# Short transfers behind the loads, and a store of 32 rows, in a cached grouped-query attention block

## The chip, the cores and the metric

The kernel runs on one core of a Trainium2 chip. A core has five instruction streams, named in the profile as PE (matrix engine; PEld is its weight load), DVE (vector), ACT (scalar), POOL and SP. SP computes nothing here: it issues transfers between HBM and the on-chip memory (SBUF). The transfers are moved by 16 DMA engines, and ACT issues two of them as well. The matrix engine writes its sums into PSUM, which is divided into banks.

The metric is device time in microseconds (us), from the first to the last instruction and a little around it. The span of the profile is the part between the first and the last instruction that was recorded.

## The reference, cut to what matters

```
x        [8, 4, 512]          bf16     B=8 sequences of 4 new tokens
k_cache  [8, 8, 2048, 128]    bf16     B, KV heads, cached tokens, head size
v_cache  [8, 8, 2048, 128]    bf16
wq       [512, 4096]          bf16
wo       [4096, 512]          bf16

q = (x @ wq).reshape(B, 4, 32, 128).transpose(0, 2, 1, 3)     # 32 query heads
k = repeat(k_cache, 4, axis=1);  v = repeat(v_cache, 4, axis=1)
p = softmax(einsum("bhqd,bhkd->bhqk", q, k) * 128**-0.5)
o = einsum("bhqk,bhkd->bhqd", p, v)
out = o.transpose(0, 2, 1, 3).reshape(B, 4, 4096) @ wo         # [8, 4, 512]
```

K and V are 33.6 MB each, wq and wo 4.2 MB each; x and the output are 32 KB each.

## The kernel before, in words

The work is cut into eight units. A unit holds four KV heads and two sequences; `units` lists them, the four pairs of sequences of the first four heads first. For a unit, K is one block of 4 MB and V another: 128 partitions, two sequences, 16 KB for each.

All large blocks pass through `ring`, a buffer with four slots of 4 MB. The order of the blocks is the list `loads`: K0, wq, K1, V0, K2, V1, K3, ..., V5, K7, V6, V7, wo. A block takes the slot of the block four places ahead of it, so its transfer waits until that one has been used up. `issue(done)` puts transfers on SP's queue as far as slots are promised; it is called once before the loop and then at the end of each pass of it (`issue(2 + 2 * u)`). Most blocks are one transfer; K0, wq, K1, V0, V1 and V7 are two; wo (`load_wo`, L113) is seven: two of 1 MB for the first half of the rows, then 1 MB, 512 KB, 256 KB and twice 128 KB. The transfers take their turn on eight completion semaphores: each transfer has one of the eight, in order of issue, and waits on its issuing engine until the transfer that had it before has landed. On one engine transfers are issued in order; a transfer that waits holds back those behind it.

`pad` is a buffer of 192 columns ahead of the ring, which nothing reads or writes.

In the loop over units, DVE turns K blocks (`turn`, L172), PE forms the scores of all heads of the unit in `s_ps`, four banks (`scores`, L195), DVE takes the maxima (`top`, L208), ACT the exponentials (`exps`, L229), DVE transposes them (L243), and ACT and POOL (in the last unit DVE too) spread them into block-diagonal weights (`weights`, L253). PE multiplies the V block of the unit before by them (`values`, L269). The last steps of a unit bring its result into the order of tokens (`scaled`, `joined`, L287, `by_tokens`, L307, `to_rows`, L321).

At the end `project` (L332) multiplies by wo. For each of 16 rows of wo in each half, two matmuls of 256 columns add up the output: the left half of the columns on partitions 0 to 31, the right half on partitions 32 to 63, both in the first bank of `s_ps`. One ACT copy (L409) brings the 64 partitions into `out_sb`, and one transfer (L411) stores 64 rows of 512 B, with a pattern of two halves by 32 tokens by 256 columns on the side of HBM.

Of the kernel before, what the change touches and what calls it, by code (L numbers as in the profile page):

```python
# [8 lines left out]
BF16 = mybir.dt.bfloat16  # L9
# [8 lines left out]
def kernel(  # L18
# [9 lines left out]
    nc = tc.nc  # L28

    B, Sq, D = x.shape  # L30
# [4 lines left out]
    T = B * Sq  # L35
# [14 lines left out]
    DH = D // 2  # L50
# [6 lines left out]
    const = ctx.enter_context(tc.tile_pool(name="const", bufs=1))  # L57
# [10 lines left out]
    pad = ring_pool.tile([128, 192], BF16, name="pad")  # L68
# [8 lines left out]
    q_bd = [const.tile([128, NB, J * 2, G, NB, Q], BF16, name=f"q_bd{i}") for i in range(2)]  # L77
    p_bd = [const.tile([128, CH // 2, G, 32, 2], BF16, name=f"p_bd{i}") for i in range(4)]
    oP = [const.tile([128, RW, T], BF16, name=f"oP{i}") for i in range(NG)]
    out_sb = const.tile([2 * T, DH], BF16, name="out_sb")  # L80

    units = [(gg, bp) for gg in range(NG) for bp in range(NP)]
    slot_of = {}
# [2 lines left out]
    def take(key):  # L86
        slot_of[key] = n_loads[0] % NS
        n_loads[0] += 1
        return slot_of[key]

    def load_kv(kind, u, parts, engines=(nc.sync,)):

        gg, bp = units[u]
        slot = take((kind, u))
        src = (k_cache if kind == "k" else v_cache)[NB * bp : NB * bp + NB, G * gg : G * gg + G]
        rows = src.rearrange("b g (s c) d -> (g s) b (c d)", c=C)
        n = C * Dh
        for i, (b0, b1, h0, h1) in enumerate(parts):
            h0, h1 = int(h0 * n), int(h1 * n)
            engines[i % len(engines)].dma_start(ring[:, slot, b0:b1, h0:h1], rows[:, b0:b1, h0:h1])  # L100

    def load_wq():
        slot = take("wq")
        rows = wq.rearrange("(p b r) n -> p b (r n)", b=NB, r=R // NB)
        for b, engine in enumerate((nc.sync, nc.scalar)):
            engine.dma_start(ring[:, slot, b, :], rows[:, b])

    def load_wo():
        slot = take("wo")
        for gg, cuts in ((0, (0, 8, RW)), (1, (0, 8, 12, 14, 15, RW))):  # L110
            rows = wo[gg * G * 512 : (gg + 1) * G * 512, :].rearrange("(p r) j -> p (r j)", r=RW)
            for r0, r1 in zip(cuts, cuts[1:]):
                nc.sync.dma_start(ring[:, slot, gg, r0 * D : r1 * D], rows[:, r0 * D : r1 * D])  # L113

    whole = [(0, NB, 0, 1)]
    by_sequence = [(b, b + 1, 0, 1) for b in range(NB)]
    by_half = [(0, NB, 0, 0.5), (0, NB, 0.5, 1)]
    loads = ["k0", "wq", ("k", 1)]
# [7 lines left out]
    def issue(done):  # L126

        while loads and n_loads[0] < done + NS:
            what = loads.pop()
            if what == "k0":  # L130
                load_kv("k", 0, by_sequence, (nc.sync, nc.scalar))
                nc.sync.dma_start(x_sb[:, :], x.flatten_outer_dims())
            elif what == "wq":
                load_wq()
            elif what == "wo":
                load_wo()
            elif what in (("k", 1), ("v", 0), ("v", 1)):
                load_kv(*what, by_sequence)
            else:
                load_kv(*what, by_half if what == ("v", NU - 1) else whole)  # L140

    issue(0)

    make_identity(nc, ident[:])
# [6 lines left out]
    for r, b in ((r, b) for r in range(rep) for b in range(NB)):  # L151
        nc.gpsimd.tensor_copy(
            out=perm[:, r, 32 - NB * Sq :]
            .rearrange("k (g x) -> k g x", g=G)[:, :, : NB * Sq]
            .rearrange("k g (b s) -> k b g s", b=NB)[:, b],
            in_=by_row[:, r, b],
        )
    for b in range(NB):
        nc.vector.tensor_reduce(
            out=of_b[:, b : b + 1],  # L160
            in_=ident[:, :].rearrange("k (g b q) -> k b g q", g=G, b=NB)[:, b],
# [27 lines left out]
    s_ps = psum_s.tile([128, NT, 512], FP32, name="s_ps")  # L189
# [138 lines left out]
    def project(gg, r0, r1):  # L328
        w = ring[:, slot_of["wo"], gg, :].rearrange("p (r j) -> p r j", r=RW)
        for r in range(r0, r1):  # L330
            for half in range(2):
                nc.tensor.matmul(  # L332
                    out_ps[half * T : (half + 1) * T, :],
                    lhsT=oP[gg][:, r, :],
                    rhs=w[:, r, half * DH : (half + 1) * DH],
                    start=(gg == 0 and r == 0),
                    stop=(gg == NG - 1 and r == RW - 1),
                )
# [9 lines left out]
    for gg in range(NG):  # L348
        psq = psum_o.tile([128, rep * Dh], FP32, tag="o", name="psq")
        for r in range(R):  # L350
# [10 lines left out]
            out=q_sb[:, gg, :, :, :, :].rearrange("t r j w e -> t (r j w e)"), in_=psq[:, :]  # L361
        )
        for i in range(rep):
            nc.vector.transpose(  # L364
                out=qT[:, gg, :, :, i, :, :].rearrange("w j b s e -> w j b (s e)").bitcast(FP32),
                in_=q_sb[:, gg, i, :, :, :].rearrange("t j w e -> t (j w e)").bitcast(FP32),
            )
    queries(0)

    out_ps = s_ps[: 2 * T, 0, :DH]  # L370
    for u in range(NU + 1):
        if u < NU:
            for t in range(NT):
# [19 lines left out]
        if u >= 1:  # L393
# [5 lines left out]
            if u == NU:  # L399
                joined(u - 1)  # L400
                by_tokens(u - 2)
        issue(2 + 2 * u)
    project(0, 0, 4)
    by_tokens(NU - 1)
    to_rows(NG - 1, RW // 4)
    project(0, 4, RW)
    project(1, 0, RW)
    assert not loads
    nc.scalar.copy(out=out_sb[:, :], in_=out_ps)  # L409
    rows = out.flatten_outer_dims().rearrange("t (h n) -> h t n", h=2)  # L410
    nc.sync.dma_start(out=rows, in_=out_sb[:, :])  # L411


# [28 lines left out]
```

## Time and profile before

| | us |
|---|---|
| median of 3 runs | 191.63 |
| lowest and highest run | 185.8, 191.71 |
| the profiled execution | 185.8 |
| its span | 183.9 |

| engine | busy us | share of the span |
|---|---|---|
| PE | 133.3 | 72% |
| DVE | 127.3 | 69% |
| ACT | 74.1 | 40% |
| POOL | 37.7 | 20% |

The rows of the profile name an engine, a line of the kernel, the operation and what is written and read (`out<-in`); a `q` behind the engine's name stands for its sequencer, which issues transfers and handles semaphores. A count is given as `x7`, a time of one instruction in ns, other times in us. In a table of stretches, each row gives the stretch, its length, the busy time of PE, PEld, DVE, ACT and POOL with the number of instructions, and at the end the granted clock of PE, the mean busy share of the 16 DMA engines and the GB/s that they moved.

### The profile page before, as it was taken

Reading aid. Unit: us, or ns where it says so; the run is one execution under the profiler, and the core shown is the slowest. Engines: PE = TensorE matmul, PEld = TensorE weight load, DVE = VectorE, ACT = ScalarE, POOL = GpSimd, SP = SyncE. Lnnn points to the kernel's source line nnn. Section 1 sums busy time; section 2 is a strip of 40 time slices with the busy share of each in tenths; the row PEclk is TensorE's granted clock in tenths of the full one; section 3 lists DMA queues with packets and bytes.
Section 4 is the critical chain, followed back from the end, with each engine's and each line's share of the span. In section 5 each row is a group of like instructions: output and inputs, shape, how many; then the busy total and the mean of one; then the engine's idle time right before and its main releaser. Section 6 shows DMA issues by size and latency. Waiting matters only on the chain.

```text
span 183.9 us, 2334 instructions
## 1 busy us (share of the span) xinstructions
PE 133.3 (72%) x900; PEld 81.4 (44%) x900; DVE 127.3 (69%) x160; ACT 74.1 (40%) x91; POOL 37.7 (20%) x98
## 2 busy tenths in 40 slices
PE   0000079901999699978996898789788968899991
PEld 0000023300358335833782377238633853398870
DVE  6527029068975997499749965997898579769140
ACT  2000020049506940793099009902980297037010
POOL 8700033008001700260034004300520040005000
PEclk9999999995699999999999999999999999999997
DMA  6999999999999999999999999999999999999980
GB/s 271 410 435 420 435 421 438 424 438 438 424 435 421 435 424 440 417 440 435 424 431 420 442 424 433 442 413 438 420 442 428 431 435 420 421 426 424 428 316 8
DMA packets 6109, 75.71 MB, mean 412 GB/s; under 512 B 498, under 2 KB 850, under 8 KB 1106
## 3 DMA queue, kind: packets, MB, share of 16 engines
q1 hardware_dynamic: 5810, 71.37, 91.1%
q10 hardware_dynamic: 288, 4.19, 5.4%
q8 instruction: 7, 0.11, 0.2%
q14 instruction: 4, 0.03, 0.0%
HBM read 75.53 MB, written 0.03 MB: 411 GB/s over the span
## 4 chain that ended last, share of the span: by engine, by line
DVE 37%; DMA 25%; PE 19%; ACT 9%; issue 3%; SPq 2%; POOL 2%; DVEq 0%; ACTq 0%; POOLq 0%
DVE kt L172 23%; DMA ring<-in_wo_dram 14%; PE s_ps L195 13%; DMA ring<-in_wq_dram 11%; ACT p_sb L229 8%; DVE stat L208 8%; PE o_ps L269 4%; DVE pt L243 2%; DVE stat L260 2%; PE psq L353 2%; SPq L113 2%; POOL p_bd L253 1%; DVE stat L216 1%; DVE o_sb L287 1%; POOL q_bd L184 1%
## 5 line engine op out<-in xcount | busy, mean ns | idle before, releaser
L195 PE MATMUL s_ps<-kt,q_bd 128*128 128x512 bf16 x256 | 67.4, 395 | 24.3 <-POOL q_bd L184 16.3
L172 DVE STREAM_TRANSPOSE kt<-ring 128x1024 f32<-128x1024 f32 x64 | 73.8, 1207 | 5.5 <-DMA ring<-in_k_cache_dram 5.2
L269 PE MATMUL o_ps<-ring,p_bd 128*128 128x256 bf16 x512 | 57.0, 273 | 0.0
L195 PEld LDWEIGHTS <-q_bd 128*128 128x128 bf16 x256 | 24.7, 99 | 66.1 <-issue 23.6
L269 PEld LDWEIGHTS <-p_bd 128*128 128x128 bf16 x512 | 49.8, 98 | 5.9
L229 ACT ACTIVATE p_sb<-s_ps,stat 128x1024 bf16<-128x1024 f32 x16 | 22.0, 1399 | 65.3 <-DVE stat L216 65.3
L253 ACT COPY p_bd<-pt 32x1024 bf16<-32x1024 bf16 x44 | 45.8, 1041 | 1.3 <-DVE pt L243 0.8
L253 POOL COPY p_bd<-pt 32x1024 bf16<-32x1024 bf16 x16 | 17.0, 1063 | 112.0 <-DVE pt L243 109.5
L208 DVE TENSOR_REDUCE stat<-s_ps 128x1 f32<-128x1024 f32 x16 | 18.8, 1219 | 12.2 <-PE s_ps L195 12.2
L243 DVE STREAM_TRANSPOSE pt<-p_sb 128x512 f32<-128x512 f32 x16 | 11.4, 711 | 16.1 <-ACT p_sb L229 16.0
L184 POOL COPY q_bd<-qT 32x64 bf16<-32x64 bf16 x64 | 13.1, 230 | 19.4 <-DVE qT L364 17.6
L344 PE MATMUL xtp<-ident,x_sb 32*128 32x32 bf16 x4 | 0.3, 194 | 14.1 <-DMA x_sb<-in_x_dram 14.1
L353 PE MATMUL psq<-ring,xT_sb 128*32 128x512 bf16 x32 | 3.6, 629 | 8.2 <-DMA ring<-in_wq_dram 8.2
L364 DVE STREAM_TRANSPOSE qT<-q_sb 128x64 f32<-128x64 f32 x8 | 1.2, 213 | 8.9 <-ACT q_sb L360 8.9
L146 DVE MEMSET p_bd<- 128x2048 uint32 x3 | 5.3, 1765 | 2.0 <-PEq L426 1.2
L344 PEld LDWEIGHTS <-x_sb 32*128 32x128 bf16 x4 | 0.2, 117 | 14.1 <-DMA x_sb<-in_x_dram 14.1
L260 DVE TENSOR_SCALAR stat<-of_b,stat 128x2 f32<-128x2 f32 x8 | 5.9, 733 | 0.3
L287 DVE SCALAR_TENSOR_TENSOR o_sb<-o_ps,stat,o_sb 128x128 bf16<-128x128 f32 x8 | 2.5, 316 | 4.8 <-ACT o_sb L281 4.8
L353 PEld LDWEIGHTS <-xT_sb 128*32 128x32 bf16 x32 | 1.3, 139 | 9.7 <-issue 9.2
L360 ACT CAST q_sb<-psq 128x512 bf16<-128x512 f32 x2 | 1.2, 586 | 10.9 <-PE psq L353 10.9
L281 ACT ACTIVATE o_sb<-o_ps,stat 128x128 bf16<-128x128 f32 x8 | 2.9, 368 | 5.6 <-PE o_ps L269 5.4
L347 ACT COPY xT_sb<-xtp 128x128 bf16<-128x128 bf16 x1 | 0.3, 266 | 11.5 <-PE xtp L344 11.5
(26 smaller groups left out, 38.4 us busy)
## 6 DMA issues: line engine op xcount, KB each, us to landing
ring<-in_k_cache_dram SPq DMA_DIRECT2D x6, 4096.0 KB, 22.0
ring<-in_v_cache_dram SPq DMA_DIRECT2D x5, 4096.0 KB, 25.3
ring<-in_v_cache_dram SPq DMA_DIRECT2D x6, 2048.0 KB, 27.1
ring<-in_k_cache_dram SPq DMA_DIRECT2D x3, 2048.0 KB, 25.4
ring<-in_wo_dram SPq DMA_DIRECT2D x3, 1024.0 KB, 25.6
ring<-in_k_cache_dram ACTq DMA_DIRECT2D x1, 2048.0 KB, 12.1
ring<-in_wq_dram ACTq DMA_DIRECT2D x1, 2048.0 KB, 20.2
ring<-in_wq_dram SPq DMA_DIRECT2D x1, 2048.0 KB, 20.9
```

Of the source, the lines that this page charges most:

```text
L146: nc.vector.memset(t[:, :, :, :, :], 0.0)
L172: nc.vector.transpose(out=kt[:, :, :, :, :].rearrange("w c j s e -> w (c j s e)").bitcast(FP32), in_=ring[:, slot_of["k", u], b, t * n : ( ...
L184: nc.gpsimd.tensor_copy(out=qb[rows, b, :, g, b, :].rearrange("w (j e) q -> w j e q", e=2), in_=qT[rows, gg, :, NB * bp + b, :, :, :].rear ...
L195: nc.tensor.matmul(s_ps[:, t, :], lhsT=q_bd[u % 2][:, b, 2 * j + e, :, :, :].rearrange("w g b q -> w (g b q)"), rhs=kts[u, b, t][:, :, j, ...
L208: nc.vector.tensor_reduce(out=stats[u][0][:, h : h + 1], in_=s_ps[:, 2 * h : 2 * h + 2, :].rearrange("q t n -> q (t n)"), axis=AX, op=ALU.max,
L229: nc.scalar.activation(out=p_sb[:, :, :, :].rearrange("q c s e -> q c e s"), in_=s_ps[:, 2 * h : 2 * h + 2, :].rearrange("q t (c e s) -> q ...
L243: nc.vector.transpose(out=pt[:, :, :, :].rearrange("s c q e -> s (c q e)").bitcast(FP32), in_=ps[u, h][:, :, :, :].rearrange("q c s e -> q ...
L253: copy(out=pb[rows, :, g, :, :], in_=pt[rows, :, :, :])
L260: nc.vector.tensor_scalar_mul(stats[u][3][:, :], of_b[:, :], stats[u][4][:, :])
L269: nc.tensor.matmul(o_pss[u][:, :, :], lhsT=pbs[u, h][:, i // 2, :, :, i % 2].rearrange("s g q -> s (g q)"), rhs=v[:, :, h * CH + i, :], st ...
L287: nc.vector.scalar_tensor_tensor(out=o_sb[:, 1, :], in0=o_pss[u][:, 1, :], scalar=stats[u][3][:, 1:2], in1=o_sb[:, 0, :], op0=ALU.mult, op ...
L353: nc.tensor.matmul(psq[g * T : (g + 1) * T, :], lhsT=xT_sb[:, r, :], rhs=w[:, (gg * G + g) * rep * Dh : (gg * G + g + 1) * rep * Dh], star ...
```

## The change

A list `probes` holds the numbers 1 to 16 in an order of its own. `load_rows` takes the next number n and transfers n rows of x, 12 columns (24 B) of each, into `pad`, each n to columns of its own; nothing reads them. It is called on SP behind each block from V0 to V6's (13 times: n = 8, 4, 12, 2, 6, 10, 14, 1, 3, 5, 7, 9, 11), and behind the first three pieces of wo (n = 13, 15, 16). As transfers, these take their turn on the eight completion semaphores like the others.

The right half of the output is now formed in the second bank of `s_ps`, still on partitions 32 to 63. ACT copies the left half, DVE the right half, into an `out_sb` of 32 partitions by 512 columns, and one transfer stores 32 rows of 1024 B.

```diff
-    out_sb = const.tile([2 * T, DH], BF16, name="out_sb")
+    out_sb = const.tile([T, D], BF16, name="out_sb")
...
+    probes = [16, 15, 13, 11, 9, 7, 5, 3, 1, 14, 10, 6, 2, 12, 4, 8]
+
+    def load_rows():
+
+        n = probes.pop()
+        nc.sync.dma_start(pad[:n, 12 * (n - 1) : 12 * n], x.flatten_outer_dims()[:n, :12])
+
     def load_wo():
...
             for r0, r1 in zip(cuts, cuts[1:]):
                 nc.sync.dma_start(ring[:, slot, gg, r0 * D : r1 * D], rows[:, r0 * D : r1 * D])
+                if probes:
+                    load_rows()
...
                 load_kv(*what, by_half if what == ("v", NU - 1) else whole)
+            if len(loads) < 15 and len(probes) > 3:
+                load_rows()
...
                 nc.tensor.matmul(
-                    out_ps[half * T : (half + 1) * T, :],
+                    out_ps[half],
...
-    out_ps = s_ps[: 2 * T, 0, :DH]
+    out_ps = [s_ps[h * T : (h + 1) * T, h, :DH] for h in range(2)]
...
-    nc.scalar.copy(out=out_sb[:, :], in_=out_ps)
-    rows = out.flatten_outer_dims().rearrange("t (h n) -> h t n", h=2)
-    nc.sync.dma_start(out=rows, in_=out_sb[:, :])
+    nc.scalar.copy(out=out_sb[:, :DH], in_=out_ps[0])
+    nc.vector.tensor_copy(out=out_sb[:, DH:], in_=out_ps[1])
+    nc.sync.dma_start(out=out.flatten_outer_dims(), in_=out_sb[:, :])
```

## The prediction

> **What bounds the kernel now.** I read the page's engine table and its 40 slices first.
>
> ```profile
> span 183.9 us, 2334 instructions
> PE 133.3 (72%) x900; PEld 81.4 (44%) x900; DVE 127.3 (69%) x160; ACT 74.1 (40%) x91; POOL 37.7 (20%) x98
> ...
> DMA  6999999999999999999999999999999999999980
> GB/s 271 410 435 420 435 421 438 424 438 438 424 435 421 435 424 440 417 440 435 424 431 420 442 424 433 442 413 438 420 442 428 431 435 420 421 426 424 428 316 8
> DMA packets 6109, 75.71 MB, mean 412 GB/s; under 512 B 498, under 2 KB 850, under 8 KB 1106
> ```
>
> No compute engine is busy for more than three quarters of the span, but the transfers are at nine tenths or more in 37 consecutive slices. Stretches of the trace, with the DMA share and GB/s as the last two numbers, give the steady rate:
>
> ```profile
> 60.00:140.00 80.00, 68.59 (x434) 40.86 (x433) 67.31 (x82) 43.85 (x52) 17.84 (x50) 1.00 1.00 429
> ```
>
> 75.71 MB at 429 GB/s is 176.5 us. Add the start and the tail after the last load, and the span is full. The chain that ended last, from 150 us on, says the same:
>
> ```profile
> 151.16 2.41 SPq L113
> 153.56 0.04 issue
> 153.61 25.58 DMA ring<-in_wo_dram
> 179.19 0.04 issue
> 179.23 0.62 PE s_ps L332 x6
> 179.85 0.01 issue
> 179.86 0.30 PE s_ps L332 x2
> 180.16 0.02 issue
> 180.19 0.37 ACT out_sb L409
> ```
>
> A piece of wo, issued at 153.61, lands 25.58 us later, because two V units and the rest of wo stand ahead of it. Earlier in the span the chain names DVE and PE, but those only decide when a slot comes free; the loads issued then join a backlog:
>
> ```profile
> ring<-in_k_cache_dram SPq DMA_DIRECT2D x6, 4096.0 KB, 22.0
> ring<-in_v_cache_dram SPq DMA_DIRECT2D x5, 4096.0 KB, 25.3
> ```
>
> 4096 KB take 9.8 us at 429 GB/s and land 22 to 25 us after issue, so 12 us or more of older work lies ahead of a typical load. The end is therefore set by three things: the bytes, what each of the 16 DMA engines does beside them, and the tail after 179.2.
>
> **The store.** This is the one part that I expect to gain. The tail in the timeline, and the transfers in it:
>
> ```profile
> 180.19 0.37 ACT L409 CAST out_sb<-s_ps 64x256 bf16<-64x256 f32 x1 [3.43 <-PE s_ps L332]
> 180.58 0.68 SPq L411 DMA_DIRECT2D out_dram<-out_sb  x1
> ```
>
> ```profile
> 179.60:181.80 2.20, 0.54 (x6) 0.15 (x3) 0.00 (x0) 0.37 (x1) 0.00 (x0) 1.00 0.00 0
> 181.80:182.75 0.95, 0.00 (x0) 0.00 (x0) 0.00 (x0) 0.00 (x0) 0.00 (x0) 0.56 0.13 34
> ```
>
> ```profile
> DMA packets 66, 0.03 MB, mean 27 GB/s; under 512 B 2, under 2 KB 66, under 8 KB 66
> ```
>
> The last fence counts the packets of 181.6 to 182.8: 64 rows of 512 B and two of under 512 B. A share of 0.13 of 16 engines is 2.1 engines: the old store is moved by two engines, 32 rows each, in 0.95 us, or 0.95 / 32 = 0.030 us a row. The new store has 32 rows of 1024 B and no outer count of two. On 16 engines each moves two rows; even at twice 0.030 us that is 0.12 us, and 0.83 us is saved. If it stayed on two engines, 16 rows each at 0.030 to 0.060 us would take 0.48 to 0.95 us and save 0 to 0.47. Only the large transfers, whose rows run over 128 partitions, show share 1.00 here; I side with them, since the factor of two stands in the old store's pattern alone: **-0.8 us**, bounds 0 and -0.83. The Trainium skill, "DMA: Bandwidth & Descriptors", section "Why a DMA increments its semaphore by 16 and not by 1", has a rule for it: the engines used are the largest number up to 16 that divides the outermost counts of both patterns. The 2.1 engines of the old store agree with it (counts 2 and 64).
>
> **The two copies.** The store now waits for ACT's copy and a DVE copy of the other half, side by side. Neither is in the trace in its new shape; both have near rows:
>
> ```profile
> L321 ACT CAST q_sb<-o_pm_m x2: 372/372/373, 125.3 to 176.4; 128x256 bf16<-128x256 f32 x2
> L321 DVE CAST q_sb<-o_pm_e x2: 416/420/425, 127.7 to 176.5; 128x256 bf16<-128x256 f32 x2
> ```
>
> ACT takes 372 ns for 128 partitions and 366 (0.37 above) for 64, so 32 do not make it shorter: a copy goes by its 256 columns. DVE's 420 ns ends 0.05 later: **+0.05 us**. DVE is idle by then (nothing on it in 179.60:181.80). The 64 projection matmuls stay as many, in the same order; writing two banks changes their 273 ns by nothing that I can price, bounds 0 either way, because the last eight wait for wo anyway.
>
> **The short rows.** Sixteen more transfers: 13 behind loads from the first V on (8, 4, 12, 2, 6, 10, 14, 1, 3, 5, 7, 9, 11 rows), three behind the first three pieces of wo (13, 15, 16). Together 136 rows of 24 B, 3.3 KB, nothing by bytes. Three prices remain.
>
> SP's queue. The waits of SP and its issues:
>
> ```profile
> SPq L100 <- DVE kt L172: 83.4, 8, 19.2
> SPq L100 <- PE o_ps L269: 39.0, 5, 7.9
> ...
> SPq L113 <- DMA ring<-in_v_cache_dram: 7.2, 2, 4.5
> ```
>
> ```profile
> L100 SPq DMA_DIRECT2D ring<-in_v_cache_dram x11: 328/368/554, 3.4 to 142.0; - x11
> ```
>
> Sixteen issues of 0.37 us are 5.9 us, on a queue that sits waiting for 83.4 + 39.0 us for slots. Each falls right behind a load, into such a wait, and the backlog of 12 us would hide a delay of 0.4 us in any case: **0**.
>
> New waits. The transfers take eight completion semaphores in turn, and each waits until the one eight before it has landed. With a short transfer between the loads, eight back is only four loads back. For K and V that is a load whose data has already been consumed, because the ring has four slots: no new wait. At the end it bites. The third piece of wo now waits for V6, the fourth for the first half of V7, the fifth for the second half, the sixth for the first piece of wo. Behind each stands the rest of wo on SP, and PE waits for those. Where the waits ended before:
>
> ```profile
> 160.20 5.18 SPq L113 DMA_DIRECT2D ring<-in_wo_dram  x2
> ```
>
> ```profile
> 165.06 0.33 SPq L113 DMA_DIRECT2D ring<-in_wo_dram  x1
> ```
>
> ```profile
> L411 SPq EVENT_SEMAPHORE  x1: 17/17/17, 169.9 to 169.9; - x1
> ```
>
> Before, the sixth piece went out at 160.20, when V6 had landed, the seventh at 165.06 with the first half of V7, and the store's wait for the second half ended at 169.9. So the new issues are at about 160.2, 165.1, 169.9, and 172.4 (2.4 us of wo later) instead of 150 to 165. At 172.4 the second to fifth pieces, 2.9 MB or 6.7 us, still stand ahead; an issue reaches its first packet in 181.8 - 180.58 = 1.2 us. The queue never runs dry: **0**, with 5 us to spare. The cover would be gone if wo moved 5 us earlier or its pieces were smaller.
>
> The engines themselves. If n rows lie on n engines, the most loaded engine gets 16 rows and 16 completion marks. No row of 24 B is in the trace. Lower bound 0, if that engine is one that finishes early:
>
> ```profile
> 177.00:178.00 1.00, 1.00 (x23) 0.92 (x20) 0.97 (x3) 0.00 (x0) 0.00 (x0) 1.00 0.90 334
> 178.00:179.00 1.00, 1.00 (x22) 0.93 (x19) 0.44 (x2) 0.00 (x0) 0.00 (x0) 1.00 0.44 163
> 179.00:179.60 0.60, 0.56 (x10) 0.25 (x7) 0.00 (x0) 0.00 (x0) 0.00 (x0) 1.00 0.18 61
> ```
>
> The share falls 0.90, 0.44, 0.18 over the last 2.6 us: some engines finish over a microsecond before the last. Upper bound by the store's rows: 32 x 0.030 = 0.96 us. Already 498 packets of under 512 B, 31 per engine, ride along at a share of 1.00, so I stay near the lower end: **+0.3 us**. Another upper bound is a row that the engine cannot overlap; it is a rival below.
>
> **Sum.** -0.8 + 0.05 + 0.3 = -0.45 us, on the profiled execution's 185.8 (span 183.9 and 1.9 around it): **185.3 us**, no change that can be told; about 2% is what a measurement of this kernel can tell. Bounds: 185.8 - 0.83 = 185.0, and 185.8 + 0.05 + 0.96 = 186.8. The median of the runs shown is 191.63, as the other two stand 5.8 us above the profiled one, which this trace cannot explain. If the changed kernel's executions divide as these do, its median reads 191.2.
>
> **Rivals.** *Slower: a short row holds its engine.* If a 24 B row is not overlapped with the 16 KB rows around it, each costs the way from issue's end (180.58 + 0.68 = 181.26) to the first packet (181.8), 0.55 us. The engine with 16 of them ends 8.8 us later, and all loads wait for their last engine: 185.8 - 0.75 + 8.8 = 193.9. It decides from (3.7 + 0.75) / 16 = 0.28 us a row. For it: no such row was seen. Against: the 31 small packets per engine at share 1.00; 0.28 us each would be 8.7 us, and 80 us at 429 GB/s have no room for that. But those are completion marks, not reads. The Trainium skill names a rule on this side: "DMA: Bandwidth & Descriptors", section "Specifications", says that transfers under 512 B are done as read-modify-write and miss the line rate. No run here shows a 24 B row.
>
> *Faster: the 5.8 us go.* The two other executions lose 191.63 - 185.8 = 5.8 us. With transfers at a share of 1.00, that would be 3.3% of the 176.5 us of transfers: engines that meet each other in some executions. Short rows that load each engine differently shift them against each other, and all executions could come out at 185.3, 3.3% under the median. Against: the last stretches show the engines 1 to 2 us apart without any help.
>
> *The change does not do what it says:* rows on other engines than n, or the store still on two: 185.0 to 186.8 again, nothing to tell.
>
> **How the numbers follow.** Forecast 0.5, and 0.07 for the store or rows laid otherwise, both within 2% like for like: 0.57 at 185.0 to 186.8, or 191.2 where the executions divide as before. Faster 0.25: 185.3 against 191.63. Slower 0.15 by the held engine at 193.9, and 0.03 for a drained queue at the end. The range runs from 184.6 (both savings whole, 0.4 for the spread between executions) to 192.2 (the 191.2 with the upper bound of the rows); it leaves out the slower cases, 0.18.
>
> **What would show it.** The store's window with a share well above 0.13 and shorter than 0.95 us; the fall of the share after 177 us no longer than 3 us; GB/s from 60 to 140 us still 429; SP's waits on V landings growing at 150 to 170 us without a hole in the DMA slices. Wrong, if GB/s drops below 415 in the middle (held engines), or if a slice before 177 us shows a gap.

## The result and the profile after

| | before | after |
|---|---|---|
| median of 17 runs each, us | 185.69 | 185.3 |
| ratio after / before | | 0.998, 95% interval 0.9972 to 0.9988 |
| profiled execution, us | 185.8 | 185.3 |
| its span, us | 183.9 | 183.3 |

The changed kernel is 0.2% faster, 0.2 to 0.5 us. That is far below the 2% which the prediction took for the least that can be told, but the interval leaves out 1: 17 runs of each tell a tenth of a per cent. Five of the 17 executions before and three of the 17 after stand 2.7 us or more above their median and are left out of the ratio, so the profiled execution was the right base for the sum.

The head of the page of the changed kernel:

```profile
span 183.3 us, 2353 instructions
PE 133.1 (73%) x900; PEld 81.3 (44%) x900; DVE 127.9 (70%) x161; ACT 74.1 (40%) x91; POOL 37.6 (21%) x98
...
DMA  6999999999999999999999999999999999999990
GB/s 232 418 443 415 447 418 443 418 440 422 436 440 411 454 415 442 415 438 422 440 422 433 425 433 438 429 425 436 422 436 436 422 436 425 417 427 425 427 369 28
DMA packets 6363, 75.72 MB, mean 413 GB/s; under 512 B 784, under 2 KB 1104, under 8 KB 1360
```

The row of transfers has no hole, and the packets under 512 B have risen from 498 to 784. The stretches of the changed kernel (PE, PEld, DVE, ACT, POOL busy, then PE's clock, DMA share, GB/s):

```profile
60.00:140.00 80.00, 68.58 (x433) 40.73 (x431) 67.29 (x82) 43.59 (x52) 17.57 (x50) 1.00 1.01 430
177.00:178.00 1.00, 1.00 (x24) 0.92 (x20) 1.00 (x4) 0.00 (x0) 0.00 (x0) 1.00 1.05 397
178.00:179.00 1.00, 1.00 (x20) 0.86 (x17) 0.34 (x2) 0.00 (x0) 0.00 (x0) 1.00 0.53 194
179.00:179.60 0.60, 0.56 (x10) 0.30 (x6) 0.00 (x0) 0.00 (x0) 0.00 (x0) 1.00 0.25 87
```

The middle moves 430 GB/s, as before. The end of its chain:

```profile
172.70 7.10 DMA ring<-in_wo_dram
179.80 0.04 issue
179.84 0.30 PE s_ps L343 x2
180.14 0.02 issue
180.16 0.37 ACT out_sb L421
180.53 0.02 issue
180.56 0.41 DVE out_sb L422
```

The last matmul ends at 180.14, against 180.16 before. All of the gain stands behind that point, and one term there went the wrong way: the DVE copy does not run beside ACT's copy, it begins 0.03 us after it ends. Its row in the timeline names ACT's copy as what released it, after 2.22 us of idling; the store follows:

```profile
180.56 0.41 DVE L422 CAST out_sb<-s_ps 32x256 bf16<-32x256 f32 x1 [2.22 <-ACT out_sb L421]
181.00 0.34 SPq L423 DMA_DIRECT2D out_dram<-out_sb  x1
```

The end of the store in the waits of SP, of the changed kernel and then of the kernel before:

```profile
SPq L449 <- DMA out_dram<-out_sb: 0.9, 1, 0.9
```

```profile
SPq L437 <- DMA out_dram<-out_sb: 1.5, 1, 1.5
```

The store is issued 0.42 us later (181.00 against 180.58), takes 0.34 instead of 0.68 us to issue, and is waited for 0.9 instead of 1.5 us. -0.34 - 0.6 + 0.42 is -0.52 us, the 0.5 by which the profiled execution is shorter.

The transfers from 180.5 to 183.3 us of the changed kernel, in 40 slices of 0.07 us:

```profile
DMA  0000000000000000000584100000000000000000
DMA packets 48, 0.03 MB, mean 12 GB/s; under 512 B 16, under 2 KB 48, under 8 KB 48
```

They are 32 rows and 16 completion marks (packets of 4 B behind the rows) in four slices, some 0.3 us where the old store took 0.95, at a share of up to 0.8, some 13 of 16 engines, where it was 0.13. This is the sign that the prediction had named.

### The profile page after: what moved, and what is told of

Its sections match the earlier page's. It is cut to its first block, busy times and chain, and to the rows that moved or that the text cites. A ratio compares the mean times of both kernels' runs of the same rounds, so it can differ in the third digit from the quotient of the medians.

```text
span 183.3 us, 2353 instructions
## 1 busy us (share of the span) xinstructions
PE 133.1 (73%) x900; PEld 81.3 (44%) x900; DVE 127.9 (70%) x161; ACT 74.1 (40%) x91; POOL 37.6 (21%) x98
## 4 chain that ended last, share of the span: by engine, by line
DVE 37%; DMA 29%; PE 17%; ACT 9%; issue 3%; POOL 2%; SPq 1%; DVEq 0%; ACTq 0%; POOLq 0%
DVE kt L183 23%; DMA ring<-in_wo_dram 18%; PE s_ps L206 13%; DMA ring<-in_wq_dram 11%; ACT p_sb L240 8%; DVE stat L219 8%; DVE pt L254 2%; DVE stat L271 2%; PE psq L364 2%; PE o_ps L280 2%; POOL p_bd L264 1%; DVE stat L227 1%; DVE o_sb L298 1%; POOL q_bd L195 1%; DVE stat L270 0%
```

## The experiments

All ratios are to the kernel before on the same chip.

**One: the new store alone.** The short transfers are left out.

```diff
-                if probes:
-                    load_rows()
...
-            if len(loads) < 15 and len(probes) > 3:
-                load_rows()
```

> The changed kernel without any of its sixteen short transfers; output in two banks, two copies, one store of 32 rows as in the change. My theory: the whole gain sits behind the last load (store issue to landing 2.5 us before, 1.5 us after; the second copy gives back 0.44 us), and the short rows cost 0.0 to 0.3 us. So 185.1 to 185.3 us, 0.4 to 0.6 below the kernel before on the same chip. Rival, the short rows themselves help (engines shifted against each other): 185.6 or more, no better than before.

Measured: 185.23 us, ratio 0.9972 (0.9961 to 0.9983), 0.3 to 0.7 us below before. So the whole gain, and a little more, is there without a short row. The packets, of this kernel:

```profile
DMA packets 6091, 75.71 MB, mean 413 GB/s; under 512 B 512, under 2 KB 832, under 8 KB 1088
```

512 packets under 512 B, where the kernel before has 498. The only transfer that differs is the store, so it leaves 14 more completion marks: 16 instead of 2. With the shares of 0.13 and up to 0.8, and one mark for each engine, the store went from two engines to sixteen.

**Two: the short rows alone.** The kernel before, with `probes`, `load_rows` and its two calls added.

> The kernel before with the sixteen short transfers alone; one bank, one copy, store of 64 rows as before. My theory: 0.0 to 0.3 us slower than before, 185.7 to 186.0 us. Rival, the short rows help: 185.3 us. Rival, a short row holds its engine by 0.55 us: about 194 us.

Measured: ratio 1.0102, interval 1.0015 to 1.0188. It rules out a gain and the 194 us, but it cannot tell 0.15% from 1.9%. It was run again:

> The kernel before with the sixteen short transfers alone, a second time, since its first interval (1.0015 to 1.0188) was too wide to tell 0.1 from 0.5%. My theory from the other runs: the short rows cost 0.05 to 0.3 us, 185.7 to 186.0 us, ratio 1.0003 to 1.0016. Rival, they cost 1% by themselves: 187.6 us.

Measured: ratio 1.0013 (1.0003 to 1.0024), that is 0.06 to 0.45 us slower. The short rows cost about 0.2 us and help nothing.

**Three: copies side by side.** No short rows; the right half is formed in a PSUM buffer of its own.

```diff
-    out_ps = [s_ps[h * T : (h + 1) * T, h, :DH] for h in range(2)]
...
+    out_r = psum_o.tile([128, NB, Dh], FP32, tag="o", name="out_r")
+    out_ps = [s_ps[:T, 0, :DH], out_r[T : 2 * T, :, :].rearrange("t b d -> t (b d)")]
```

> No short transfers; the right half of the output is formed in a PSUM buffer of its own instead of the second bank of the scores' buffer, so that the DVE copy waits for PE and not for the ACT copy. My theory: the DVE copy, which began at 180.56 behind ACT's, begins at about 180.16, and the store is issued 0.4 us earlier: 184.8 us, 0.4 below the two-copies kernel without short rows. Rival, the copies meet on PSUM or the store is bound by something else: 185.2 us.

Measured: 184.69 us, ratio 0.9953 (0.994 to 0.9967). The end of its timeline:

```profile
180.29 0.36 ACT L418 CAST out_sb<-s_ps 32x256 bf16<-32x256 f32 x1 [3.49 <-PE out_r L339]
180.33 0.41 DVE L419 CAST out_sb<-out_r 32x256 bf16<-32x256 f32 x1 [1.85 <-PE out_r L339]
180.81 0.35 SPq L420 DMA_DIRECT2D out_dram<-out_sb  x1
```

Both copies now wait for PE and run together; from the start of the first to the store's issue it is 0.52 us, where the changed kernel takes 181.00 - 180.16 = 0.84, and the first experiment as much. The ratio falls by another 0.0019, 0.35 us, in step with these 0.32, though the two intervals overlap; the rows of the timeline decide. The delay of the DVE copy was thus a wait in the program, which went when the two copies read two PSUM buffers instead of two banks of one, and no limit of the engines.

**Four: the old copy, two stores.** The kernel before, its one bank and one ACT copy; the store is cut in two.

```diff
-    rows = out.flatten_outer_dims().rearrange("t (h n) -> h t n", h=2)
-    nc.sync.dma_start(out=rows, in_=out_sb[:, :])
+    for h, engine in enumerate((nc.sync, nc.scalar)):
+        engine.dma_start(out=out.flatten_outer_dims()[:, h * DH : (h + 1) * DH], in_=out_sb[h * T : (h + 1) * T, :])
```

> The kernel before, with one bank and one ACT copy, no short transfers; the store is cut into two transfers of 32 rows of 512 B, one issued by SP and one by ACT. If the gain of the change is the number of engines that move the store, this has it without the second copy: store issued at 180.6 as before, landing about 1.5 us later instead of 2.5, 184.7 to 184.9 us. Rival, the gain came from the copies, the banks or the longer rows: 185.6 us.

Measured: 184.86 us, ratio 0.9955 (0.994 to 0.997). Its timeline and its packets:

```profile
180.01 0.36 ACT L409 CAST out_sb<-s_ps 64x256 bf16<-64x256 f32 x1 [3.52 <-PE s_ps L332]
180.40 0.35 SPq L411 DMA_DIRECT2D out_dram<-out_sb  x1
180.40 0.39 ACTq L411 DMA_DIRECT2D out_dram<-out_sb  x1
```

```profile
DMA packets 6139, 75.71 MB, mean 414 GB/s; under 512 B 528, under 2 KB 880, under 8 KB 1136
```

The rows are still 512 B, and neither the banks nor the copies have changed; the store is two transfers, issued side by side, and the outer count of two is gone from each. 528 is 30 marks more than before: 32 instead of 2, 16 for each transfer. That gives 0.8 us, as much as the third experiment and more than the change. Either version beats both kernels; their intervals do not tell them apart.

**Five: 31 rows in each short transfer.**

```diff
-        nc.sync.dma_start(pad[:n, 12 * (n - 1) : 12 * n], x.flatten_outer_dims()[:n, :12])
+        nc.sync.dma_start(pad[:31, 12 * (n - 1) : 12 * n], x.flatten_outer_dims()[:31, :12])
```

> The changed kernel with 31 rows in each of the sixteen short transfers instead of 1 to 16. 31 shares no divisor but 1 with the numbers up to 16: if the number of engines goes by divisors, all 31 rows, 496 in total, lie on one engine. My theory, a short row costs an engine 10 to 30 ns and nothing else: that engine ends 5 to 15 us later, less up to 2 us by which it may have been early: 188 to 199 us, and the share of the transfers falls to about one engine of 16 at the end. Rival, a short row holds its engine by 0.55 us: over 400 us. Rival, the rows are spread over all engines whatever their number: 185.3 to 185.8 us.

Measured: 188.49 us, ratio 1.0124 with an interval of 0.9985 to 1.0262. It settles the rival of 400 us and not that of rows spread over all engines. Again:

> The changed kernel with 31 rows in each short transfer, a second time, for a profile of an undisturbed execution. My theory: 496 rows on one engine at about 9 ns, 4.5 us, of which 1 to 3 us are spare on that engine: 187 to 188.5 us, with a share of about one engine of 16 (0.06) in the last 2 us before the store. Rival, the time is lost evenly on all engines: the share falls from 1.0 to 0 within a microsecond.

Measured: 187.16 us, ratio 1.0082 (1.0053 to 1.0111). Its packets, and the stretches at its end:

```profile
DMA packets 6603, 75.72 MB, mean 410 GB/s; under 512 B 1024, under 2 KB 1344, under 8 KB 1600
```

```profile
179.00:180.00 1.00, 0.66 (x14) 0.47 (x12) 0.00 (x0) 0.00 (x0) 0.00 (x0) 1.00 0.18 65
180.00:181.00 1.00, 0.93 (x14) 0.61 (x14) 0.00 (x0) 0.00 (x0) 0.00 (x0) 1.00 0.06 23
```

Packets under 512 B: 1024 - 512 = 512 more than with no short transfer, 496 rows and 16 marks, one mark for each transfer: each lay on one engine. And the end shows it: a share of 0.06 for a whole microsecond is one engine of 16 at work alone. The kernel loses 1.9 us against the changed one (1.0082 - 0.9980, of 185.7). That is 4 ns for each of the 480 rows that this engine has more, and only a lower bound of the price, as the engine may have had time to spare. The price itself is in the trace. The packets of 160.47 to 160.65 us:

```profile
DMA packets 41, 0.08 MB, mean 459 GB/s; under 512 B 31, under 2 KB 31, under 8 KB 31
```

The 31 short ones are the rows of one transfer, one behind the other on their engine: 0.18 us over 31 is 5.8 ns a row. 480 of them are 2.8 us, of which 1.9 show, so 0.9 would be what the engine had to spare.

**Six: 32 rows in each.** The same line with 32.

> The changed kernel with 32 rows in each of the sixteen short transfers: two rows on each of 16 engines if the number of engines goes by divisors, 32 rows in total on each. My theory, 10 to 30 ns each: 185.3 to 186.0 us. Rival, held engine: 32 x 0.55 = 17.6 us more, 203 us.

Measured: 185.55 us, ratio 0.999 (0.9979 to 1.0002), 0.3 us more than the first experiment. Its packets:

```profile
DMA packets 6859, 75.73 MB, mean 413 GB/s; under 512 B 1280, under 2 KB 1600, under 8 KB 1856
```

1280 - 512 = 768 more: 512 rows and 256 marks, 16 engines for each transfer. Here no engine is left out, as each gets 32 rows and 16 marks; 0.33 us (0.9990 - 0.9972, of 185.7) over 48 is 7 ns each; with intervals of 0.2 us on either ratio it may be 1 to 13, and the 5.8 ns of the trace lie in it. A row held for 0.55 us is out by a factor of some 80.

**Seven: three short transfers behind each load.** 16 rows of 4 B each, from V0 to V6, none behind wo.

```diff
-            if len(loads) < 15 and len(probes) > 3:
-                load_rows()
+            if len(loads) < 15 and len(loads) > 1:
+                for _ in range(3):
+                    load_rows()
...
-        nc.sync.dma_start(pad[:n, 12 * (n - 1) : 12 * n], x.flatten_outer_dims()[:n, :12])
+        nc.sync.dma_start(pad[:16, 2 * i : 2 * i + 2], x.flatten_outer_dims()[:16, :2])
```

> Three short transfers of 16 rows of 4 B behind each load from V0 to V6, none behind wo; output as in the change. Eight transfers back is now two loads back, so a load is issued when the one two ahead of it has landed, with one load (9.8 us) still in the queue. My theory: waits of SP on landings grow, but the queue never runs dry: 185.3 to 186.0 us. Rival, each further transfer costs about 0.5 us on the path: 39 of them, about 205 us.

Measured: 185.91 us, ratio 1.0 (0.9986 to 1.0015). SP's longest waits, and the transfers of the middle:

```profile
SPq L100 <- DMA ring<-in_k_cache_dram: 48.9, 6, 9.6
SPq L100 <- DMA ring<-in_v_cache_dram: 40.9, 6, 8.1
```

```profile
60.00:140.00 80.00, 68.55 (x432) 40.62 (x430) 67.28 (x82) 43.42 (x52) 17.48 (x49) 1.00 1.01 428
```

SP waits 48.9 + 40.9 = 89.8 us for landings, and the engines are at a share of 1.01 all the same: one load still queued covers the waits. The kernel is 0.5 us slower than the first experiment (1.0000 - 0.9972, of 185.7), which the packets can account for: each engine has 39 more rows and 39 more marks, and 78 at 5.8 ns, if a row of 4 B and a mark cost what a row of 24 B does, are 0.45 us.

**Eight: seven behind each load.** The same with 7.

> Seven short transfers of 16 rows of 4 B behind each load from V0 to V6, none behind wo; output as in the change. Eight transfers back is the load just ahead, so each load waits until the one before it has landed and the queue runs dry: at least 1.2 us from issue to first packet plus the landing, for some 13 loads. My theory: 202 to 213 us, with holes in the row of transfers, where three short ones cost nothing. Rival, the price goes by the number of short transfers: 7/3 of what three behind each load cost.

Measured: 227.58 us in the median of four, 223.97 in the profiled execution. The issues of SP, and four stretches (DMA share and GB/s at the end):

```profile
68.08 0.39 SPq L100 DMA_DIRECT2D ring<-in_k_cache_dram  x1
68.51 3.38 SPq L114 DMA_DIRECT2D pad<-in_x_dram  x7
81.41 0.39 SPq L100 DMA_DIRECT2D ring<-in_v_cache_dram  x1
81.84 3.30 SPq L114 DMA_DIRECT2D pad<-in_x_dram  x7
93.56 0.39 SPq L100 DMA_DIRECT2D ring<-in_k_cache_dram  x1
```

```profile
78.00:79.00 1.00, 1.00 (x10) 0.65 (x7) 0.58 (x4) 0.99 (x2) 0.36 (x1) 1.00 1.07 459
79.00:80.00 1.00, 0.00 (x1) 0.00 (x0) 0.00 (x0) 0.99 (x2) 0.94 (x3) 1.00 0.37 107
80.00:81.00 1.00, 0.00 (x0) 0.00 (x0) 0.00 (x0) 0.98 (x2) 0.88 (x5) 1.00 0.06 17
81.00:82.00 1.00, 0.00 (x0) 0.00 (x0) 0.63 (x1) 0.99 (x2) 0.47 (x3) 1.00 0.00 0
```

The holes are there, and the step from three to seven is no price per short transfer: three cost 0.5 us over the first experiment, so 7/3 of it would be 1.2, and seven cost 38 us over the kernel before (223.97 against 185.8). But the time lies above the 202 to 213 us expected, because my figure for a hole was too small. Loads are issued 13.3 and 12.2 us apart where their bytes take 9.8, so a hole is 2.4 to 3.5 us and not 1.2 and a little. The packets of 79.7 to 82.4 us show why:

```profile
DMA packets 61, 0.02 MB, mean 6 GB/s; under 512 B 60, under 2 KB 60, under 8 KB 60
```

A packet counts where it begins. Only one of the 61 is a row of a load (0.02 MB), and it is in the stretch from 80 to 81, where the share of 0.06 is about one engine of 16. All other rows have begun by 79.7; one engine works on alone, and only the landing of its row releases the next issue, at 81.41.

## Why the prediction was right, step by step

*The bound.* Right: 429 and 430 GB/s before and after, no hole, and the last matmul at the same time within 0.02 us.

*The store,* -0.8 us. Right in kind and a little small: the marks (498 to 512) show two engines becoming sixteen, and without the copies' wait it is worth 0.84 us (fourth experiment, 0.0045 of 185.7) to 0.87 us (third). In the trace the store by itself gains 0.94 us, more than my bound of 0.83: 0.6 in the wait for its landing, where I had 0.8 from the rows, and 0.34 in the issue, which fell from 0.68 to 0.34 us and which I had not counted. The rule of the Trainium skill, "DMA: Bandwidth & Descriptors", section "Why a DMA increments its semaphore by 16 and not by 1", that the engines are the largest number up to 16 dividing the outermost counts, agrees with each count here: 2 for the old store, 16 for the new, n for n rows (784 - 512 = 272 = 136 rows + 136 marks), 1 for 31, 16 for 32.

*The two copies,* +0.05 us. Wrong: 0.45 us in the trace, from the start of the first copy to the issue of the store (0.84 against 180.58 - 180.19 = 0.39), and 0.35 us of it came back in the third experiment's ratio. The step that failed is "side by side": I took the DVE copy's duration from its near row (420 ns; it took 415) and did not ask what it waits for. The trace names ACT as what releases it, not PE. The row of the older pair of copies (L321), which I used for the durations, read two PSUM buffers, and there the pair did run together.

*The short rows,* +0.3 us. Right in kind, a little large: 0.24 us (0.06 to 0.45) alone in the old kernel, and 0.15 us in the new one (0.9980 - 0.9972), a difference within the two intervals. In my sum one engine had 16 rows and 16 marks; at the 5.8 ns of the fifth experiment these are 0.19 us, where I had allowed up to 30 ns for a row. SP's queue at 0 and the new waits at 0 were right: SP's waits on V's landings in front of wo grew from 7.2 to 17.4 us,

```profile
SPq L120 <- DMA ring<-in_v_cache_dram: 17.4, 3, 8.8
```

and no slice shows a gap; the third and fourth pieces of wo went out at 160.09 and 164.96 us, where I had forecast 160.2 and 165.1. Experiments seven and eight show how much cover that had: with loads two back it still held, with one back it was gone.

*The sum.* -0.45 us forecast, -0.37 us measured. That it came so close is luck, since errors cancel: the copies cost 0.4 us more than in the sum, the store gained 0.14 us more (0.94) and the rows cost 0.15 us less.

*The rivals.* The held engine fell in every run with short rows: 5.8 ns a row in the trace of the fifth experiment against the 280 that would have decided. The Trainium skill, "DMA: Bandwidth & Descriptors", section "Specifications", says that transfers under 512 B miss the line rate because of a read-modify-write. The trace of the fifth experiment agrees on the rate, with 24 B in 5.8 ns, 4 GB/s, where an engine's part of the 429 is 27; the read-modify-write no run here shows. But a row below the rate is not a held engine. The faster rival fell with the second experiment: rows that load the engines differently bring no gain. Its 3.3% had been reckoned from the median of three runs, 191.63, and that of 17 is 185.69.

## What to carry to other kernels

Where the transfers fill the span, look at what stands behind the last one: a store whose pattern began with a count of two ran on two engines here, and cutting it into two transfers was worth as much as reshaping the output. Two copies by two engines run side by side only if the program lets them; read what each waits for before counting them as parallel, and give each a PSUM buffer of its own. An extra short transfer cost next to nothing here in bytes or time, but it takes a turn on the completion semaphores, and the price came at once when the one waited for was the load just ahead.

## What was not expected of the hardware

A transfer that waits for its predecessor's landing pays for the spread of the engines as well. In the eighth experiment the holes were 2.4 to 3.5 us, though an issue reached its first packet in 1.2 us in the kernel before: one engine began its last row after 80 us, when all other rows had begun by 79.7.

The issue itself can become long. Four issues of the kernel with 31 rows on one engine (second run):

```profile
95.05 3.45 SPq L100 DMA_DIRECT2D ring<-in_v_cache_dram  x1
112.97 5.34 SPq L100 DMA_DIRECT2D ring<-in_v_cache_dram  x1
130.89 7.22 SPq L100 DMA_DIRECT2D ring<-in_v_cache_dram  x1
149.09 8.86 SPq L113 DMA_DIRECT2D pad<-in_x_dram  x1
```

From 95.05 to 130.89 us each load of K and V holds SP for 3.4 to 7.3 us, and at 149.09 a short transfer holds it for 8.86, where 0.32 to 0.45 us is usual in the changed kernel. But this is not a matter of the short transfers alone. The kernel before has no such transfer and two long issues, of 2.41 us (in the prediction's chain) and of 3.91 us, both for wo while V6 and V7 were still on their way:

```profile
153.61 3.91 SPq L113 DMA_DIRECT2D ring<-in_wo_dram  x1
```

So an issue may wait for room in a queue, and rows on one engine may fill that engine's part of it first. No run here was made to show that, and the cause stays open.
